# Block-sparse attention into an FFT-gated layer on one Trainium2 core: earlier masks, smaller transform steps, rationed loads, outputs turned by TensorE

## Chip, core and metric

The kernel runs on one core of one Trainium2 chip, in one launch. The metric is the device time of the whole program in microseconds (us), as a median over runs. The profile is of one execution on that core.

## What is computed

Two layers follow each other. The first is causal attention on 4 batches, 8 heads, 768 positions and head width 64, in which every query sees its own block of 64 keys and the best three blocks by a gate score (query times mean key of the block). The second takes the joined heads (768 x 512 per batch), projects them three ways, convolves the second projection with a filter over the sequence by an FFT, multiplies the three, and projects again:

```
gate_scores = einsum('bhsd,bhnd->bhsn', q, k_mean_of_block)      # causal blocks only
mask        = own block | top 3 blocks, and pos_q >= pos_k
attn        = softmax(where(mask, q @ k.T / sqrt(64), -1e9)) @ v
x           = attn, heads joined                                  # (4, 768, 512)
x1, x2, x3  = split(x @ w_proj, 3)
conv        = irfft(rfft(x2) * rfft(filter))                      # over the 768 positions
out         = (x1 * conv * x3) @ w_out
```

## The kernel before

**The unit of work.** Heads are taken in pairs: 16 pairs, numbered p, four to a batch. Each head's 768 x 768 causal scores are computed in three groups of 896 columns, so a pair has six groups and the program has 96 slots (`slots`), six to a pair and 24 to a batch. Slot n of the main loop (L642) issues, in this order: the score matmuls of slot n+1 (`scores`, L371), the exponential of slot n on ScalarE (L387, written `ex`) and its triangular cut on GpSimd (L390), the transfers that were put off (`flush`), the list `early[n]`, one step of the second layer, the product matmuls of slot n-1 with V (`products`, L396), further steps, and the list `bank[n]`. All engines run their instructions in the order in which the program issues them. Below, n0 = 6p is the first slot of pair p.

**Preparing a pair.** K and Q arrive as rows (`load`, L75) and are turned by TensorE (L269, tiles `kt`, `qt`). ScalarE casts them (L282 to `KH`, L316 to `TQ`); VectorE takes block sums of the keys (L285, `krs`), makes the gate's right side from them (`prep_kr`, L301 to L305, `bd` and `kr`) and keeps the rounding rest of the queries (L318, `ql`). `prep_gate` (L324) multiplies them into the gate scores `g`; `prep_mask` (L337) finds the third best per query on VectorE (L342, `m`) and writes 0/1 masks (`MN`). `prep_turn` (L350) turns the masks on TensorE (L354, `mt`) and ScalarE writes them as 44 extra rows beside the queries (L355, into `TQ`). The score matmuls then have 76 rows to sum over, 64 of the head and 12 of the mask (L378). The first head of a pair reads `TQ` and `KA`, the second `QB` and `KB`; SyncE's transfers copy `KH` into `KA` and `KB` (L291, L292) and the second head's rows from `TQ` into `QB` (L322 for the queries, L357 for the masks). L355 overwrites rows that L322 reads.

**Where these steps stand.** A table by slot sets it (L611 to L630): for p > 1 loads of k, q, v at n0-15, n0-13, n0-11, `prep_k` at n0-9 and n0-7, `prep_q` at n0-6 and n0-5, `prep_kr` at n0-5, `prep_gate` at n0-4, `prep_mask` at n0-3, `prep_turn` in `bank` of slot n0-2. The scores of slot n0 are issued at the start of slot n0-1, so on TensorE they come straight behind the turned masks.

**Out of the attention.** After a head's third group, VectorE divides by the sums (L416, L417, `xnat`). After a pair, a transposing transfer on SyncE's queue (L431) turns it to `xT`, and `fold` (L435, two VectorE operations, L438 and L439, at slot 6p+9) adds and subtracts the mirrored halves (`xf`). Only the last pair is turned by TensorE (L428, copied by ScalarE, L429).

**The second layer** (`hyena`, L442) of batch b runs as a list of steps in the slots of batch b+1, from the fifth on, each step with a cost in a credit scheme: six projections `x2` (L459), eight `gates` (x1 and x3, L518 and L521), three transforms `fft` (cosine and sine half, six matmuls into two PSUM tiles, then four VectorE products L477 to L481), four inverses and six outputs (L533). The last batch's list runs at the end, with nothing beside it, on the score tiles of PSUM (`sc_tile`, two buffers).

**The first batch** has no second layer beside it. Its slots from 2 on hold a list (`filler`, L559): cosines from sines, the filter folded (L227, fp32 matmuls, tile `rev`, into `fil`), its spectrum (`spectrum`, L245: six matmuls into two PSUM tiles, ScalarE scaling one and VectorE combining, L240 and L241, into `Asb`, `Bsb`, `A2`), and the turned transform matrices (L231). The six filter transfers (L210, L211) are issued before slot 0, the weights `wp` in four pieces in slots 2 to 8. The sine table itself is made before slot 0 (L114 to L136: products on TensorE, rounding on VectorE and GpSimd, a sum on VectorE, L131, sine on ScalarE, L132).

Of the kernel before, what the change touches and what calls it, by code (L numbers as in the profile page):

```python
# [18 lines left out]
def kernel(  # L19
# [43 lines left out]
    staging = ctx.enter_context(tc.tile_pool(name="staging", bufs=1))  # L63
# [60 lines left out]
    def sine_whole(i):  # L124
        pr, ka = sine[i]
        nc.gpsimd.tensor_scalar(ka, in0=ka, scalar1=-MAGIC, scalar2=-float(S2),
                                op0=ALU.add, op1=ALU.mult)

    def sine_rest(i):
        pr, ka = sine.pop(i)  # L130
        nc.vector.tensor_add(ka, pr, ka)  # L131
        nc.scalar.activation(FS[:, i, :], ka, AF.Sin, bias=0.0, scale=TWO_PI / S2)  # L132

    nc.scalar.activation(tw, twf, AF.Sin, bias=0.0, scale=math.pi / S)
    for i in range(HC):
        sine_products(i)  # L136
    sel = const.tile([P, 2], FP32, name="sel")
# [3 lines left out]
    for i in range(HC):  # L141
        sine_whole(i)
# [51 lines left out]

    sgn = const.tile([P, 1], FP32, name="sgn")
# [17 lines left out]
    def load_wp(dc):  # L213
        nc.gpsimd.dma_start(wp[:, dc, :], moe_w_proj[dc * P:(dc + 1) * P, :])
# [16 lines left out]
    def turn_matrix(dst, src, j):  # L231
        pt = one("pt", (P, HC, P), fp)
        for i in range(HC):
            nc.tensor.transpose(pt[:, i, :], src[:, i, P * j:P * (j + 1)], id16)
        (nc.scalar.copy if dst is IC else nc.vector.tensor_copy)(
            dst[:, j, :], pt.rearrange("p i t -> p (i t)"))

    def turned(dst, first, s0, second, s1, op):
# [6 lines left out]
    def spectrum(j, part):  # L245
        sl = slice(P * j, P * (j + 1))
        if part == 0:
            spec[j] = hcp, hsp = one("hcps"), one("hsps")
            for i in range(HC):
                nc.tensor.matmul(hcp, lhsT=FC[:, i, sl], rhs=fil[:, 0, i, :],  # L250
                                 start=(i == 0), stop=(i == HC - 1))
            for i in range(HC):
                nc.tensor.matmul(hsp, lhsT=FS[:, i, sl], rhs=fil[:, 1, i, :],
                                 start=(i == 0), stop=(i == HC - 1))
            turned(Asb[:, j, :], hcp, tw[:, 0, j:j + 1], hsp, tw[:, 1, j:j + 1], ALU.add)
            cosB = tw0[:, 0:1] if j == 0 else tw[:, 0, j:j + 1]
            turned(Bsb[:, j, :], hsp, cosB, hcp, tw[:, 1, j:j + 1], ALU.subtract)
            if j == 0:
                turned(A2, hcp, tw0[:, 0:1], hsp, tw0[:, 1:2], ALU.add)
# [13 lines left out]
    def prep_k(p, t):  # L273
# [14 lines left out]
        for f in ((cast, sums) if t == 0 else (sums, cast)):  # L288
            f()
# [8 lines left out]
    def prep_kr(p):  # L298
        krs = state.pop(("krs", p))
        bd = small.tile([P, 2, NB], FP32, name="bd", tag="bd")  # L300
        nc.vector.tensor_tensor(bd, krs.unsqueeze(1).to_broadcast([P, 2, NB]),  # L301
                                sel.unsqueeze(2).to_broadcast([P, 2, NB]), op=ALU.mult)
        kr = small.tile([P, 2, 2, NB], fp, name="kr", tag="kr")
        nc.vector.tensor_copy(kr[:, 0], bd)
        nc.vector.tensor_sub(kr[:, 1], bd, kr[:, 0])  # L305
# [90 lines left out]
    def products(n):  # L396
# [14 lines left out]
        if g == NS - 1:  # L411
# [8 lines left out]
            if h == 1:  # L420
# [4 lines left out]
                if p == NP - 1:  # L425
                    xt = one("xt", (P, S), fp)
                    for c in range(SC):
                        nc.tensor.transpose(xt[:, P * c:P * (c + 1)], xn[:, c, :], id16)  # L428
                    nc.scalar.copy(xT[:, dc, :], xt)  # L429
                else:  # L430
# [11 lines left out]
    def hyena(b, spread):  # L442
# [20 lines left out]
        def fft(j):  # L463
            x2eo, PQ = st["x2"], st["PQ"]
            sl = slice(P * j, P * (j + 1))
            xc, xs = two("xc", "xs")
# [3 lines left out]
            for i in range(HC):  # L470
                nc.tensor.matmul(xs, lhsT=FS[:, i, sl], rhs=x2eo[:, 1, i, :],
                                 start=(i == 0), stop=(i == HC - 1))
            t1 = hy2.tile([P, Dm], FP32, name="t1", tag="t1")
            t2 = hy2.tile([P, Dm], FP32, name="t2", tag="t2")
            t3 = hy2.tile([P, Dm], FP32, name="t3", tag="t3")
            t4 = hy2.tile([P, Dm], FP32, name="t4", tag="t4")
            nc.vector.tensor_mul(t1, xc, Asb[:, j, :])  # L477
            nc.vector.tensor_mul(t4, xc, Bsb[:, j, :])  # L478
# [237 lines left out]
```

## Time and profile before

| | us |
|---|---|
| median of 3 runs | 327.16 |
| lowest, highest | 324.58, 331.69 |
| the profiled execution, device time | 325.43 |
| the profiled execution, span from first to last instruction | 323.7 |
| busy in the span: TensorE / VectorE / ScalarE / GpSimd | 250.3 / 183.9 / 174.7 / 131.1 |

In the profile PE is TensorE's matmuls, PEld its weight loads, DVE VectorE, ACT ScalarE, POOL GpSimd, SP SyncE, and SPq or POOLq the transfers that SyncE's or GpSimd's queue issues. A wait is written as engine, tile and line, then what ended the wait. The busy share is an average over stages: the start, the 24 slots of the first batch, 72 slots with the second layer beside them, and the last batch's second layer by itself.

### The profile page before, as it was taken

The numbers are of one execution on the slowest core, as the hardware profiler recorded it, in microseconds if no ns is written. First come the engines' busy times: TensorE is split into PE (matmuls) and PEld (weight loads), VectorE is DVE, ScalarE is ACT, GpSimd is POOL, SyncE is SP. The second block draws the span as 40 slices with busy tenths as digits, with TensorE's granted clock in tenths as the row PEclk, the third lists the DMA queues.
The fourth block names the chain that finished last, engine by engine and source line by source line (L and its number), as shares of the span: only waits on it lengthen the run. The fifth ranks groups of instructions, "written<-read, shape, count | busy, mean of one in ns | idle before, by whom it ended". The sixth has DMA issues, their size and how long they took to land.

```text
span 323.7 us, 6068 instructions
## 1 busy us (share of the span) xinstructions
PE 250.3 (77%) x2171; PEld 154.0 (48%) x2171; DVE 183.9 (57%) x561; ACT 174.7 (54%) x277; POOL 131.1 (40%) x227
## 2 busy tenths in 40 slices
PE   5378657728698978897979778979897789888675
PEld 3254334516464545654545445546454455444332
DVE  3566256433463858585438676765386758136650
ACT  3551356727477445666965365759753566431224
POOL 6753012221331365464312555552226557203680
PEclk9996598966769999999999999999999999999999
DMA  9699648494584927262968262649640201310005
GB/s 172 108 261 225 143 90 167 94 181 101 121 187 85 140 53 156 55 138 54 258 168 160 53 130 56 138 81 258 175 100 4 61 4 25 132 67 0 2 0 194
DMA packets 96943, 37.20 MB, mean 115 GB/s; under 512 B 88785, under 2 KB 92561, under 8 KB 96913
## 3 DMA queue, kind: packets, MB, share of 16 engines
q1 hardware_dynamic: 95808, 34.72, 48.5%
q0 software_dynamic: 1104, 2.10, 3.9%
q8 instruction: 17, 0.28, 0.4%
q14 instruction: 14, 0.11, 0.1%
HBM read 24.64 MB, written 6.29 MB: 96 GB/s over the span
## 4 chain that ended last, share of the span: by engine, by line
PE 33%; DVE 25%; ACT 13%; issue 10%; DMA 6%; POOL 4%; DVEq 0%; POOLq 0%; ACTq 0%
PE sps L378 5%; PE op L533 5%; ACT ex L387 3%; ACT TQ L355 3%; DMA xT<-xnat 3%; PE x1p L518 3%; PE x3p L521 3%; PE o L408 3%; DVE gg L526 3%; PE x2p L459 3%; DVE t L477 2%; DVE t L478 2%; ACT KH L282 2%; DVE m L342 2%; DVE krs L285 2%
## 5 line engine op out<-in xcount | busy, mean ns | idle before, releaser
L390 POOL TENSOR_SCALAR_AFFINE_SELECT ex<-ex 128x256 f16<-128x256 f16 x96 | 40.8, 427 | 122.8 <-ACT ex L387 103.4
L387 ACT ACTIVATE ex<-sps 128x896 f16<-128x896 f32 x96 | 88.3, 925 | 1.4 <-PE sps L378 1.0
L408 PEld LDWEIGHTS <-ex 128*128 128x128 f16 x672 | 34.5, 102 | 32.3 <-DVE xnat L417 17.6
L408 PE MATMUL o<-V,ex 128*128 128x65 f16 x672 | 39.2, 200 | 11.0 <-DVE xnat L417 10.7
L378 PE MATMUL sps<-TQ,KA 76*128 76x512 f16 (+1 forms) x144 | 29.7, 322 | 21.9 <-ACT TQ L355 18.8
L282 ACT CAST KH<-kt 128x384 f16<-128x384 f32 x32 | 15.3, 478 | 46.0 <-DVE krs L285 25.0
L285 DVE TENSOR_REDUCE krs<-kt 128x6 f32<-128x384 f32 x32 | 17.5, 552 | 33.2 <-PE kt L269 27.3
L480 POOL TENSOR_TENSOR PQ<-t,t 128x512 f16<-128x512 f32 x12 | 15.2, 1265 | 41.1 <-DVE t L479 41.1
L378 PEld LDWEIGHTS <-KA 76*128 76x128 f16 x144 | 15.1, 106 | 33.1 <-issue 28.9
L378 PE MATMUL sps<-QB,KB 76*128 76x512 f16 (+1 forms) x144 | 28.1, 306 | 0.5 <-ACT ex L387 0.3
L355 ACT ACTIVATE TQ<-mt 44x768 f16<-44x768 f16 x16 | 12.9, 805 | 24.7 <-PE mt L354 18.5
L533 PE MATMUL op<-wo,yT 128*128 128x512 f16 x96 | 23.7, 379 | 2.0 <-POOL yT L489 2.0
L459 PE MATMUL x2p<-wp,xf 128*128 128x512 f16 x96 | 24.0, 379 | 1.1 <-DVE xf L438 0.8
L521 PE MATMUL x3p<-xT,wp 128*128 128x384 f16 x96 | 19.5, 325 | 4.8 <-ACT x1sb L524 3.4
L526 DVE TENSOR_TENSOR gg<-x1sb,x3p 128x384 f32<-128x384 f16 x24 | 13.2, 552 | 17.1 <-PE x3p L521 9.6
L518 PE MATMUL x1p<-xT,wp 128*128 128x384 f16 x96 | 19.5, 325 | 3.9 <-DVE t L478 3.9
L316 ACT ACTIVATE TQ<-qt 128x384 f16<-128x384 f32 x32 | 15.7, 497 | 11.2 <-PE qt L269 11.1
L489 POOL TENSOR_TENSOR yT<-gg,yy 128x384 f16<-128x384 f32 x16 | 15.9, 995 | 13.7 <-DVE yy L506 13.7
L269 PE MATMUL kt<-id,k_nat 128*128 128x128 f32 x96 | 19.3, 323 | 1.0 <-DMA k_nat<-in_k_dram 1.0
L318 DVE SCALAR_TENSOR_TENSOR ql<-qt,TQ 128x256 f16<-128x256 f32 (+1 forms) x32 | 15.4, 486 | 7.6 <-ACT TQ L316 7.6
L536 ACT COPY osb<-op 128x512 f32<-128x512 f32 x24 | 14.2, 590 | 10.1 <-PE op L533 10.1
L521 PEld LDWEIGHTS <-wp 128*128 128x128 f16 x128 | 12.4, 97 | 15.0 <-issue 7.3
(145 smaller groups left out, 487.9 us busy)
## 6 DMA issues: line engine op xcount, KB each, us to landing
k_nat<-in_k_dram SPq DMA_DIRECT2D x32, 192.0 KB
q_nat<-in_q_dram SPq DMA_DIRECT2D x32, 192.0 KB
v_nat<-in_v_dram SPq DMA_DIRECT2D x32, 192.0 KB
out_dram<-osb SPq DMA_DIRECT2D x24, 256.0 KB
KA<-KH SPq DMA_DIRECT2D x16, 96.0 KB
KB<-KH SPq DMA_DIRECT2D x16, 96.0 KB
QB<-TQ SPq DMA_DIRECT2D x16, 96.0 KB
wp<-in_moe_w_proj_dram POOLq DMA_DIRECT2D x4, 384.0 KB, 5.6
```

Of the source, the lines that this page charges most:

```text
L282: nc.scalar.copy(kh[:, F * t:F * (t + 1)], kt)
L285: nc.vector.tensor_reduce(out=krs[:, 6 * t:6 * t + 6], in_=kt.rearrange("p (n j) -> p n j", j=64), axis=AX.X, op=ALU.add)
L355: nc.scalar.activation(tq[64:108, :], mt[64:108].rearrange("p c s -> p (c s)"), AF.Copy, bias=0.0, scale=MQ)
L378: nc.tensor.matmul(t[:, col:col + q1 - q0], lhsT=kk[0:64 + NB, P * kc:P * (kc + 1)], rhs=qq[0:64 + NB, q0:q1], start=True, stop=True, skip ...
L387: nc.scalar.activation(ex, t[:, 0:W], AF.Exp, bias=0.0, scale=EXPS)
L390: nc.gpsimd.affine_select(out=tri, in_=tri, compare_op=ALU.is_ge, fill=0.0, base=0, pattern=[[0, 2], [1, P]], channel_multiplier=-1)
L408: nc.tensor.matmul(o[:, qc, :], lhsT=ex[:, c0:c0 + P], rhs=V16[p % 3][:, kc, h, 0:65], start=first, stop=False, skip_group_check=True)
L459: nc.tensor.matmul(pa, lhsT=xf[:, eo, dc, P * i:P * (i + 1)], rhs=wp[:, dc, Dm:2 * Dm], start=(dc == 0), stop=(dc == DC - 1))
L518: nc.tensor.matmul(x1p, lhsT=wp[:, d2, dsl], rhs=xT[:, d2, hs], start=(d2 == 0), stop=(d2 == DC - 1))
L521: nc.tensor.matmul(x3p, lhsT=wp[:, d2, 2 * Dm + P * dc:2 * Dm + P * (dc + 1)], rhs=xT[:, d2, hs], start=(d2 == 0), stop=(d2 == DC - 1))
L526: nc.vector.tensor_mul(g, x1sb, x3p)
L533: nc.tensor.matmul(op, lhsT=st["yT"][:, cc, P * i:P * (i + 1)], rhs=wo[:, cc, :], start=(cc == 0), stop=(cc == DC - 1))
```

## The change

It has six parts.

1. **Pair schedule.** `prep_k` at n0-10 and n0-8, `prep_q` at n0-7 and n0-6, `prep_kr` at n0-7 and (for p > 0) on GpSimd, gate and mask together at n0-5, `prep_turn` at n0-3; loads at n0-17, n0-13, n0-9; `fold` at 6p+10. Where VectorE and ScalarE both read a turned key tile, ScalarE's cast comes first (for p > 0).
2. **Transform in halves.** `fft(j)` becomes `fft(j, 0)` and `fft(j, 1)`, each with one PSUM tile and two VectorE products. In the last batch each half has a whole score tile.
3. **First batch's transfers.** Before slot 0 stand only k, v, q of the next pairs; the three pairs of filter transfers go to slots 2, 4, 6; `wp` goes in 12 pieces of one third, from slot 9 on; `wo` at slot 30.
4. **Filter spectrum in steps.** One half per slot is multiplied and copied out of PSUM (`hsb`), GpSimd scales and VectorE combines from these copies some slots later; the filler list becomes a table by slot. The staging tiles share memory with tiles of the second layer.
5. **First outputs turned by TensorE.** Pairs 0 to 3 take no transposing transfer; `turn_x` (slot 6p+8) turns them on TensorE and VectorE copies them out.
6. **Start.** The rounded part of the sine is added in PSUM by a matmul with a scaled identity (`idn`) and all three sines come before the first keys; `prep_kr(0)` stands before `prep_q(0)`.

```diff
@@ sine
-        nc.vector.tensor_add(ka, pr, ka)
-        nc.scalar.activation(FS[:, i, :], ka, AF.Sin, bias=0.0, scale=TWO_PI / S2)
+        kw = hy2.tile([P, F], fp, name="dft_kw", tag="x1sb")
+        nc.gpsimd.tensor_scalar(kw, in0=ka, scalar1=-MAGIC, scalar2=1.0, op0=ALU.add, op1=ALU.mult)
+        nc.tensor.matmul(pr, lhsT=idn, rhs=kw, start=False, stop=True, skip_group_check=True)
+        nc.scalar.activation(FS[:, i, :], pr, AF.Sin, bias=0.0, scale=TWO_PI / S2)
@@ spectrum
+    def spectrum(j, which):
+        sl = slice(P * j, P * (j + 1))
+        hps = one("hps")
+        for i in range(HC):
+            nc.tensor.matmul(hps, lhsT=(FC, FS)[which][:, i, sl], rhs=fil[:, which, i, :],
+                             start=(i == 0), stop=(i == HC - 1))
+        spec[j, which] = hsb = hy2.tile([P, Dm], FP32, name="hsb", tag=f"h{which}")
+        (nc.scalar.copy if which else nc.vector.tensor_copy)(hsb, hps)
...
+        nc.gpsimd.tensor_scalar(t, in0=second, scalar1=s1, scalar2=0.0, op0=ALU.mult, op1=ALU.add)
         nc.vector.scalar_tensor_tensor(out=dst, in0=first, scalar=s0, in1=t, op0=ALU.mult, op1=op)
@@ prep_kr
+        e = nc.gpsimd if p else nc.vector
...
@@ turn_x
+    def turn_x(p):
+        b, dc = divmod(p, DC)
+        xn, xT = xns[p], xTs[b]
+        xt = one("xt", (P, S), fp)
+        for c in range(SC):
+            nc.tensor.transpose(xt[:, P * c:P * (c + 1)], xn[:, c, :], id16)
+        (nc.scalar.copy if p == NP - 1 else nc.vector.tensor_copy)(xT[:, dc, :], xt)
@@ fft
+            xx = single("xx")
             for i in range(HC):
-                nc.tensor.matmul(xc, lhsT=FC[:, i, sl], rhs=x2eo[:, 0, i, :],
+                nc.tensor.matmul(xx, lhsT=(FC, FS)[which][:, i, sl], rhs=x2eo[:, which, i, :],
...
@@ table by slot
-            at(early, n0 - 15, lambda p=p: load(p, "k"))
-            at(early, n0 - 11, lambda p=p: load(p, "v"))
-            at(bank, n0 - 9, lambda p=p: prep_k(p, 0))
...
-        at(early, n0 - 5, lambda p=p: prep_kr(p))
-        at(bank, n0 - 4, lambda p=p: prep_gate(p))
-        at(early, n0 - 3, lambda p=p: prep_mask(p))
-        at(bank, n0 - 2, lambda p=p: prep_turn(p))
-        at(early, n0 + 3, lambda p=p: fold(p - 1))
+            at(early, n0 - 17, lambda p=p: load(p, "k"))
+            at(early, n0 - 9, lambda p=p: load(p, "v"))
+            at(bank, n0 - 10, lambda p=p: prep_k(p, 0))
...
+            at(early, n0 - 7, lambda p=p: prep_kr(p))
+            at(bank, n0 - 5, lambda p=p: gate_mask(p))
+            at(bank, n0 - 3, lambda p=p: prep_turn(p))
+        if p < DC:
+            at(bank, n0 + 8, lambda p=p: turn_x(p))
+        at(early, n0 + 10, lambda p=p: fold(p))
+        fills[10 + 2 * j].append(lambda j=j: filter_fold(j))
+        fills[16 + 4 * j].append(lambda j=j: spectrum(j, 0))
+        fills[17 + 4 * j].append(lambda j=j: spectrum(j, 1))
```

**TensorE at the end of the mask turn of a pair in the second batch, before.** `MN` are the masks, `KA` and `TQ` the first head's keys and queries, and the three score matmuls are those of the pair whose masks were just turned.

```order
L354 LDWEIGHTS MN_159
L354 MATMUL mt<-id_171,MN_159 128x128
L378 LDWEIGHTS KA_164
L378 MATMUL sps<-TQ_168,KA_164 128x512
L378 LDWEIGHTS KA_164
L378 MATMUL sps<-TQ_168,KA_164 128x128
L378 LDWEIGHTS KA_164
L378 MATMUL sps<-TQ_168,KA_164 128x256
```

The same place now; `KB` and `QB` belong to the second head of the pair before:

```order
L361 LDWEIGHTS MN_167
L361 MATMUL mt<-id_179,MN_167 128x128
L385 LDWEIGHTS KB_173
L385 MATMUL sps<-QB_177,KB_173 128x384
L385 LDWEIGHTS KB_173
L385 MATMUL sps<-QB_177,KB_173 128x128
L385 LDWEIGHTS KB_173
L385 MATMUL sps<-QB_177,KB_173 128x384
```

A whole slot of other work (another pair's scores, a step of the second layer, products) now stands between the turned masks and the scores that read them.

**SyncE's queue behind the first pair's query copy, before.** `fa` and `fb` are the filter's halves, `KA_164` to `QB_170` the second pair's operands.

```order
L357 DMA QB_169<-TQ_167 12x768
L80 DMA v_nat<-in_v_dram 128x6x64 x2
L210 DMA fa<-in_moe_filter_fft_dram 128x512
L211 DMA fb<-in_moe_filter_fft_dram 128x512
L210 DMA fa<-in_moe_filter_fft_dram 128x512
L211 DMA fb<-in_moe_filter_fft_dram 128x512
L210 DMA fa<-in_moe_filter_fft_dram 128x512
L211 DMA fb<-in_moe_filter_fft_dram 128x512
L80 DMA k_nat<-in_k_dram 128x6x64 x2
L80 DMA q_nat<-in_q_dram 128x6x64 x2
L291 DMA KA_164<-KH_200 64x768
L292 DMA KB_166<-KH_200 64x768
```

The same place now, as far as the second pair's query copy (`QB_178`, L329):

```order
L79 DMA k_nat<-in_k_dram 128x6x64 x2
L79 DMA v_nat<-in_v_dram 128x6x64 x2
L79 DMA q_nat<-in_q_dram 128x6x64 x2
L364 DMA QB_177<-TQ_175 12x768
L297 DMA KA_172<-KH_209 64x768
L298 DMA KB_174<-KH_209 64x768
L79 DMA k_nat<-in_k_dram 128x6x64 x2
L329 DMA QB_178<-TQ_176 64x768
L211 DMA fa<-in_moe_filter_fft_dram 128x512
L212 DMA fb<-in_moe_filter_fft_dram 128x512
```

The six filter transfers and one load moved from ahead of the second pair's operands to behind its query copy.

## Rows read from the trace of the kernel before

**Rows 1.** The page, 40 equal slices: granted clock, share of the DMA engines.
```profile
PEclk9996598966769999999999999999999999999999
DMA  9699648494584927262968262649640201310005
```

**Rows 2.** Timeline of ACT (start, us, engine, line; in brackets the wait before).
```profile
15.83 0.92 ACT L387 ACTIVATE ex<-sps 128x896 f16<-128x896 f32 x1 [0.99 <-PE sps L378]
...
34.35 0.81 ACT L355 ACTIVATE TQ<-mt 44x768 f16<-44x768 f16 x1 [5.21 <-DMA QB<-TQ]
...
73.47 0.81 ACT L355 ACTIVATE TQ<-mt 44x768 f16<-44x768 f16 x1 [6.37 <-PE mt L354]
...
89.61 0.92 ACT L387 ACTIVATE ex<-sps 128x896 f16<-128x896 f32 x1
...
273.70 0.92 ACT L387 ACTIVATE ex<-sps 128x896 f16<-128x896 f32 x1
```

**Rows 3.** Windows: stretch, length, busy PE, PEld, DVE, ACT, POOL, granted clock, DMA.
```profile
15.83:89.61 73.78, 48.31 (x428) 32.79 (x427) 35.78 (x126) 37.13 (x56) 19.84 (x40) 0.78 0.75 154
89.61:96.00 6.39, 6.24 (x63) 4.63 (x61) 4.21 (x21) 4.68 (x9) 2.55 (x5) 0.59 0.80 175
96.00:273.70 177.70, 151.82 (x1441) 94.29 (x1439) 115.40 (x348) 109.82 (x175) 79.44 (x117) 1.00 0.50 108
```

**Rows 4.** Waits of PE, 96 to 275 us (in total, times, longest).
```profile
PE sps L378 <- ACT TQ L355: 10.7, 11, 1.2
PE x1p L518 <- DVE t L478: 3.9, 6, 0.8
...
PE ye L498 <- DVE lt L345: 1.8, 2, 0.9
PE x3p L521 <- DVE t L481: 1.0, 3, 0.3
```

**Rows 5.** The chain that ended last, in order of time (start, us, what).
```profile
28.46 5.79 DMA QB<-TQ
...
62.53 6.93 DMA xT<-xnat
```

**Rows 6.** Transfers from 8 to 20 us, in 40 slices.
```profile
GB/s 217 219 218 218 219 215 220 216 242 226 257 143 164 108 67 21 0 0 0 0 0 0 0 0 0 0 0 31 31 22 141 207 281 261 257 221 186 219 266 410
```

**Rows 7.** Instructions by line and form, whole span (busy us, mean ns, idle before).
```profile
L461 DVE CAST x2eo<-x2p 128x512 f16<-128x512 f32 x12 | 8.3, 688 | 5.9 <-PE x2p L459 5.9
...
L304 DVE CAST kr<-bd 128x24 f16<-128x24 f32 x16 | 4.5, 279 | 0.5
...
L126 POOL TENSOR_SCALAR dft_ka<-dft_ka 128x384 f32<-128x384 f32 x3 | 1.5, 509 | 0.9 <-DVE dft_ka L120 0.8
...
L429 ACT COPY xT<-xt 128x768 f16<-128x768 f16 x1 | 0.8, 798 | 1.0 <-PE xt L428 1.0
...
L428 PE MATMUL xt<-id,xnat 128*128 128x128 f16 x6 | 0.5, 221 | 0.9 <-DVE xnat L417 0.9
```

**Rows 8.** Timeline: the fold's first operation early, and late with POOL beside it.
```profile
53.62 0.35 DVE L438 TENSOR_TENSOR xf<-xT 128x384 f16<-128x384 f16 x1
...
271.05 0.99 POOL L489 TENSOR_TENSOR yT<-gg,yy 128x384 f16<-128x384 f32 x1 [0.96 <-DVE yy L506]
...
271.35 0.92 DVE L438 TENSOR_TENSOR xf<-xT 128x384 f16<-128x384 f16 x1
```

**Rows 9.** Timeline of the start, PE and POOL.
```profile
10.47 0.40 PE L333 MATMUL g<-kr,TQ 128*128 128x24 f16 x2 [2.28 <-DVE kr L304]
...
11.39 0.82 POOL L173 TENSOR_SCALAR_AFFINE_SELECT KA<-KA 12x768 f16<-12x768 f16 x1
...
14.89 0.59 PE L378 MATMUL sps<-TQ,KA 76*128 76x512 f16 x1 [0.95 <-ACT TQ L355]
```

**Rows 10.** Timeline of DVE in the last batch's second layer.
```profile
302.19 0.69 DVE L477 TENSOR_TENSOR t<-sps,Asb 128x512 f32<-128x512 f32 x1 [1.15 <-PE sps L471]
```

**Rows 11.** Waits of DVE, 100 to 275 us.
```profile
DVE krs L285 <- PE kt L269: 19.7, 5, 4.8
```

More of the change, by code (lines that the diff above doesn't have):

```diff
@@ L136 @@
         sine_products(i)
+    idn = const.tile([P, P], fp, name="idn")
+    nc.gpsimd.tensor_scalar(idn, in0=id32, scalar1=-float(S2), scalar2=0.0, op0=ALU.mult, op1=ALU.add)
+    for i in range(HC):
+        sine_rest(i)
     sel = const.tile([P, 2], FP32, name="sel")
@@ L234, in turn_matrix @@
             nc.tensor.transpose(pt[:, i, :], src[:, i, P * j:P * (j + 1)], id16)
[L235 to L238 removed]
+        nc.vector.tensor_copy(dst[:, j, :], pt.rearrange("p i t -> p (i t)"))
+    spec = {}
+    def spectrum(j, which):
+        sl = slice(P * j, P * (j + 1))
+        hps = one("hps")
+        for i in range(HC):
+            nc.tensor.matmul(hps, lhsT=(FC, FS)[which][:, i, sl], rhs=fil[:, which, i, :],
+                             start=(i == 0), stop=(i == HC - 1))
+        spec[j, which] = hsb = hy2.tile([P, Dm], FP32, name="hsb", tag=f"h{which}")
+        (nc.scalar.copy if which else nc.vector.tensor_copy)(hsb, hps)
@@ L241, in turned @@
         nc.vector.scalar_tensor_tensor(out=dst, in0=first, scalar=s0, in1=t, op0=ALU.mult, op1=op)
-    spec = {}
[L245 to L259, printed above, removed]
@@ L287, in sums @@
                                     axis=AX.X, op=ALU.add)
-        for f in ((cast, sums) if t == 0 else (sums, cast)):
-            f()
+        if p == 0 and t == 0:
+            sums()
+            state["cast"] = cast
+        else:
+            cast()
+            sums()
+            if p == 0:
+                state.pop("cast")()
         if t == 1:
@@ L424, in products @@
                 xT, xf = xTs[b], xTs["f", b]
[L425 to L430, printed above, removed]
+                if p >= DC and p < NP - 1:
                     late.append(lambda: nc.sync.dma_start_transpose(
@@ L557, in make_flip @@
             fill=1.0, base=-(P - 1), pattern=[[1, P]], channel_multiplier=1)
-    def filler():
-        first = [lambda: cosines()]
-        first += [lambda i=i: filter_fold(i) for i in range(HC)]
-        first += [lambda j=j: spectrum(j, 0) for j in range(HC)]
-        first += [lambda j=j: (turn_matrix(IC, FC, j), turn_matrix(IS, FS, j)) for j in range(HC)]
-        return first
     def flush():
@@ L573 @@
     prep_k(0, 1)
-    flush()
-    sine_rest(0)
+    prep_kr(0)
     prep_q(0, 0)
     prep_q(0, 1)
+    nc.scalar.preload_act_table_set("natural_log_exp_and_others")
+    prep_gate(0)
+    prep_mask(0)
     flush()
-    sine_rest(1)
-    prep_kr(0)
-    prep_gate(0)
-    sine_rest(2)
-    nc.vector.memset(MN[0], 0.0)
-    prep_mask(0)
-    nc.scalar.preload_act_table_set("natural_log_exp_and_others")
+    load(2, "k")
+    load(1, "v")
+    load(2, "q")
     prep_turn(0)
-    flush()
     nc.gpsimd.tensor_copy(KB[0][64:64 + NB, :], erow)
@@ L590 @@
     prep_v(0)
-    load(1, "v")
-    for i in range(HC):
-        load_filter(i)
     scores(0)
@@ L651 @@
             queue += hyena(b - 1, True)
-        if b == 0:
-            if m >= 2 and spread_filler:
-                spread_filler.pop(0)()
-        else:
+        for f in fills[n]:
+            f()
+        if b:
             credit += 28.2 / per * 1.03
```

125 lines of the change are left out of this document (74 added, 51 removed).

## Prediction

> **What bounds the kernel now.** I read the page's slices first. In [rows 1] the granted TensorE clock is below full speed only in the first twelve slices, the start and the first batch; from then on it is full. So the time is not of one kind, and I cut it by the exponentials, of which there is one per slot: slot 0 begins at 15.83 us, slot 24 at 89.61, slot 95 at 273.70 [rows 2]. The first 24 slots take 73.8 us, 3.07 each, the other 72 take 184.1 us, 2.56 each, although only the latter have the second layer beside them. The rest is 15.8 us of start and 50.0 us of tail (323.7 - 273.70).
>
> The windows say what each stretch lacks [rows 3]. In the first batch no engine is full: TensorE is busy 48.3 of 73.8 us, and that at a mean clock of 0.78; ScalarE 37.1, VectorE 35.8. It is bound by waits. The two longest on ScalarE are of the masks' writing: 5.2 us until the second pair's query copy has landed, and 6.4 us until a mask turn is done [rows 2]. The chain says what lies behind them [rows 5]: that copy took 5.8 us on its way, behind the filter in SyncE's queue, and a transposing transfer took 6.9 us; `fold` waits for such a transfer in VectorE's queue, and `prep_mask` stands behind `fold`. From 96 us on TensorE is busy 151.8 of 177.7 us, 85%: it is the bound, and what can go is its waits. The largest is the one for the masks, 10.7 us in 11 waits of about 1 us [rows 4].
>
> **The change part by part.** The sum is made against the profiled execution: 325.43 us, of which 323.7 are span and 1.7 lie around it. It is 1.7 us below the median of the runs, 327.16, and I add that at the end.
>
> *Start.* The gate waits 2.3 us for the first pair's `kr`, which VectorE makes after two sine operations and the query rests [rows 9]. Now it comes before these. Three small matmuls and two sines on ScalarE come ahead of the first keys instead. The scores of slot 0, at 14.89 us, also need the key rows that GpSimd finishes at 12.2 (11.39 + 0.82), so no more than 2.3 us can go, and a loss of 1 us is possible if the sines hold up the key cast. I take -1.0.
>
> *First batch.* What it would take if no wait stood out is bounded by work. TensorE's 48.3 us at a clock of 0.78 are 37.7 at full clock (an estimate: not all of a matmul's time goes with the clock); three outputs turned by six transposes, 0.5 us each time [rows 7], make it 39.2. VectorE: 35.8, less four times three small `kr` operations (0.28 the longest kind), 3.3, plus three copies of a turned output, 0.8 each by ScalarE's row, plus three copies of half a spectrum, 0.69 each by that of `x2eo` [rows 7]: 37.0. ScalarE loses seven scalings and gains three copies, and stays below. At the 85% that TensorE reaches later the batch would take 39.2 / 0.854 = 45.9 us. The other floor is the transfers. The window moved 154 GB/s for 73.8 us [rows 3], 11.4 MB; saturated by the same kind of loads the queue moved 215 to 220 GB/s [rows 6], so these bytes need 52 us. Three transposing transfers leave and one load goes ahead of slot 0, but the loads of the next pairs stay. The ends are thus 45.9 and, if nothing comes of it, 73.8; I take 53, next to the floor of the transfers: -20.8. The named waits fit this. The second pair's query copy is now behind one load instead of three filter pairs and two loads, so the 5.2 us go; the transposing transfer, and with it the 6.4 us, is gone; mask, fold and turn stand in different slots. Late next is the wait for the transfers themselves.
>
> *Slots 24 to 95.* Between the mask turn and the scores that read it TensorE now has a slot of other work, some 2.5 us against a wait of 1; ScalarE's 0.8 us for L355 falls in it. All 10.7 us of [rows 4] are open; some will come back as waits for ScalarE and VectorE, which are reached later than TensorE in each slot, and I keep 8. The waits for the transform's products (3.9 and 1.0) shrink because each half gives its one PSUM tile back after two products instead of four: I keep 2.5. Of the 1.8 us behind the mask's `lt` I keep 1. In the 6.4 us from 89.61 the clock was 0.59 [rows 3]; 6.24 busy us there are 3.7 at full clock, 4.3 at 85%: -2. Against this, the fold of a batch's last pair now stands in the slot of the first `x2` step, which TensorE reaches before VectorE is done: three times one or two operations, 0.35 us each alone and 0.92 beside GpSimd [rows 8], so 0.4 to 1.8 us; I take 1.2, +3.6. `prep_kr` on GpSimd is not in the trace: three operations of 0.28 us on VectorE, at most 0.5 (the larger tile of L126) on GpSimd, twelve pairs; GpSimd is busy 45% of the stretch, and the gate comes two slots later, so nothing. If that cover failed it would be up to 1.5 us a pair, 18 us. Sum -9.9, say -10, with ends of 0 and -16.
>
> The Trainium skill speaks against two of these moves (page "SBUF — State Buffer", section "SBUF: two separate sides"): VectorE and GpSimd share one port pair, a VectorE operation with two SBUF inputs and a GpSimd operation lock each other out for a whole instruction. Seven spectrum operations now read both inputs from SBUF, and their partner moved to GpSimd. The trace agrees with the rule, the 0.35 us against 0.92 of [rows 8]. By it each of the seven could wait for one GpSimd scaling, an estimate of 0.7 us, and the sum would be 4.8 us longer; without it, nothing. TensorE and the transfers are the floor there, so my sum has nothing for it.
>
> *Tail.* VectorE is the bound in the three transforms at the end, and waits before the second and third: 1.15 us in [rows 10], 1.1 in the other like it, because a transform's first product waits for both halves. With halves it can begin after three matmuls of six. Half a score tile is given away by each, so the ring turns faster: 0 to -2.3, I take -1.5.
>
> Sum: 325.4 - 1.0 - 20.8 - 10 - 1.5 = 292.1, and with 1.7 for the median 293.8: **294 us**.
>
> **The rivals.** *The clock stays low in the first batch.* The clock fell after stretches in which TensorE stood idle [rows 1, 3]. If the first batch keeps such gaps, its 39.2 us of work at full clock become up to 78 at half, and the batch takes its 73.8 us as before: 294 + 20.8 = 315. For it: without the second layer TensorE has 39 us of work in 53, less than later. Against it: the gaps of several microseconds are those that have names above, and the change removes what they wait for.
>
> *The waits only change their names.* The mask's place behind other work is of use only if no other wait is nearly as late. ScalarE casts, scales and exponentiates in order, VectorE drains in order, and in each slot both come after TensorE. If the slot is paced by these, the first batch's 20.8 and the 8 of the masks come back: 294 + 28.8 = 323, no change. For it: in the first batch three engines are within a few per cent of each other in work. Against it: all three are half idle there.
>
> *Slower: VectorE stands before the gate.* `prep_mask` now follows `prep_gate` in the same slot, so VectorE's next instruction waits until TensorE has come through a step, the products and the gate. Behind it in VectorE's queue stand the drains of the next slot, which give TensorE its PSUM tiles back. The price is a wait like that for turned keys, 19.7 us in 5, 3.9 each [rows 11], put on TensorE twelve times: 47 us, against 33 gained, which gives 294 + 47 = 341. It decides from 2.8 us a pair on (33 / 12). Against it: those 19.7 us stood in the trace while TensorE was 85% busy, so VectorE waits ahead of TensorE, not behind it.
>
> **How the numbers follow.** The forecast with its own range, 280 to 307, has 0.68; the low clock, 315, has 0.14; changed names, 323, 0.06; VectorE before the gate, 0.06; better than 280 (the first batch at 46 and all later waits gone: 325.4 - 2.3 - 27.9 - 16 - 2.3 + 1.7 = 279), 0.06. The range from 280 to 315 leaves out 0.18. A measurement of this kernel can tell about 2% from no change, so "faster" begins below 320.6: 0.68 + 0.14 + 0.06 = 0.88; same 0.06; slower 0.06.
>
> **What would show it.** In the profile after: slot 24's exponential at about 68 us; no wait of 5 us before L355's successor in the first batch; a granted clock of 0.9 or more there; the wait of the score matmuls for the masks' writing under 3 us in all; about 2.4 us a slot from slot 24 on; a new wait of `x2p` for `xf` three times. I am wrong if the first batch still takes over 65 us, if the later slots keep 2.56 us, or if the mask search waits for the gate by more than a microsecond a pair.

## Result, and the profile after

The changed kernel took 289.38 us, the median of four runs (287.29 to 290.83), against 328.75 for the kernel before in the same comparison: a ratio of 0.8875, with its 95% interval [0.8764, 0.8986]. The same file run again in a later comparison took 285.17 (284.17 to 291.76), ratio 0.8722 [0.8674, 0.8769]. Forecast were 294 us and a range of 280 to 315. The profiled execution took 290.83 us, of which 289.1 are span.

The stretches are cut as before, by the exponentials of slots 0, 24, 48 and 95. This table carries the rest of the text (us; "again" is the same kernel's second profile):

| | before | forecast of the change | after | change | again |
|---|---|---|---|---|---|
| start, to slot 0 | 15.83 | -1.0 | 15.71 | -0.1 | 15.45 |
| first batch, slots 0 to 23 | 73.8 | -20.8 | 53.5 | -20.3 | 51.5 |
| slots 24 to 95 | 184.1 | -10 | 166.7 | -17.4 | 166.6 |
| of these, slots 48 to 95 | 120.2 | | 105.6 | -14.6 | 105.6 |
| tail, from slot 95 | 50.0 | -1.5 | 53.2 | +3.2 | 50.2 |
| span | 323.7 | | 289.1 | -34.6 | 283.7 |

The page's slices of after, which answer to [rows 1]:

```profile
PEclk9997988977779999999999999999999995999998
DMA  9997898997907965568774735796512011300005
```

The granted clock still dips in the first twelve slices, and there is a new dip in slice 34, at the start of the tail, where before had none. The timeline of ScalarE answers to [rows 2]:

```profile
13.91 0.81 ACT L362 ACTIVATE TQ<-mt 44x768 f16<-44x768 f16 x1 [2.88 <-DMA QB<-TQ]
...
15.71 0.92 ACT L394 ACTIVATE ex<-sps 128x896 f16<-128x896 f32 x1 [0.99 <-PE sps L385]
...
38.93 0.81 ACT L362 ACTIVATE TQ<-mt 44x768 f16<-44x768 f16 x1 [2.33 <-DMA QB<-TQ]
...
69.19 0.91 ACT L394 ACTIVATE ex<-sps 128x896 f16<-128x896 f32 x1
...
235.91 0.92 ACT L394 ACTIVATE ex<-sps 128x896 f16<-128x896 f32 x1
```

The masks' writing (L355 before, L362 now) waited 5.21 and 6.37 us in the first batch; the longest left are 2.88, in the start, and 2.33. The windows answer to [rows 3] (columns: length, busy PE, PEld, DVE, ACT, POOL, granted clock, DMA share, GB/s):

```profile
15.71:69.19 53.48, 43.09 (x436) 30.85 (x435) 33.48 (x118) 33.01 (x50) 26.72 (x61) 0.87 0.85 168
69.19:130.33 61.14, 53.95 (x524) 35.16 (x522) 42.77 (x125) 38.53 (x63) 35.75 (x62) 0.94 0.65 126
75.54:235.91 160.37, 150.43 (x1472) 96.99 (x1468) 111.49 (x331) 110.79 (x177) 87.86 (x152) 0.98 0.57 126
130.33:235.91 105.58, 100.20 (x996) 64.16 (x995) 72.91 (x217) 75.87 (x122) 56.91 (x101) 1.00 0.54 128
235.91:246.00 10.09, 7.43 (x44) 3.41 (x44) 2.19 (x6) 3.47 (x6) 2.33 (x4) 0.68 0.13 52
```

For slots 48 to 95 the row of before is

```profile
153.54:273.70 120.16, 103.30 (x990) 64.23 (x987) 77.43 (x237) 75.92 (x121) 53.46 (x80) 1.00 0.49 113
```

There TensorE's idle time fell from 16.9 us (120.16 - 103.30) to 5.4 (105.58 - 100.20): it is 95% busy now, at the upper level of its clock (2.4 GHz) in both. Its waits from 75.54 us on, which answer to [rows 4]:

```profile
PE x2p L469 <- DVE xf L448: 2.7, 3, 2.2
PE x3p L533 <- ACT x1sb L536: 1.7, 3, 0.6
PE op L545 <- POOL yT L501: 1.7, 2, 0.9
PE sps L385 <- ACT ex L394: 1.6, 3, 0.7
PE o L415 <- DVE xnat L424: 1.5, 3, 0.5
```

The wait for the masks, 10.7 us in 11 before, is not in the list any more, nor are those for the transform's products. The wait of `x2p` for the fold (`xf`) is there three times, as forecast.

### The profile page after: what moved, and what is told of

The parts are those of the page before. It is cut to its first block, busy times and chain, and to the rows that moved or that the text cites. A ratio compares the mean times of both kernels' runs of the same rounds, so it can differ in the third digit from the quotient of the medians.

```text
span 289.1 us, 6157 instructions
## 1 busy us (share of the span) xinstructions
PE 245.6 (85%) x2198; PEld 153.9 (53%) x2198; DVE 176.3 (61%) x523; ACT 170.4 (59%) x270; POOL 148.7 (51%) x288
## 4 chain that ended last, share of the span: by engine, by line
PE 56%; DVE 12%; ACT 11%; POOL 9%; issue 5%; DMA 5%; SPq 1%; ACTq 0%; DVEq 0%; POOLq 0%
PE sps L385 8%; PE op L545 7%; PE x2p L469 6%; PE x3p L533 5%; PE o L415 5%; PE x1p L530 5%; ACT ex L394 4%; DMA QB<-TQ 3%; PE kt L269 3%; PE qt L269 3%; PE xx L481 3%; ACT TQ L362 2%; POOL yT L501 2%; DVE xnat L424 2%; DMA k_nat<-in_k_dram 2%
## 5 line engine op out<-in xcount | busy, mean ns | idle before, releaser
L397 POOL TENSOR_SCALAR_AFFINE_SELECT ex<-ex 128x256 f16<-128x256 f16 x96 | 39.9, 418 | 84.5 <-ACT ex L394 78.4
L415 PEld LDWEIGHTS <-ex 128*128 128x128 f16 x672 | 33.8, 100 | 25.0 <-DVE xnat L424 9.4
L415 PE MATMUL o<-V,ex 128*128 128x65 f16 x672 | 37.9, 198 | 5.7 <-DVE xnat L424 5.1
L385 PE MATMUL sps<-TQ,KA 76*128 76x512 f16 (+1 forms) x144 | 28.4, 310 | 4.9 <-DMA k_nat<-in_k_dram 2.1
L492 POOL TENSOR_TENSOR PQ<-ta 128x512 f16<-128x512 f32 x12 | 15.2, 1269 | 31.3 <-DVE ta L491 31.2
L545 PE MATMUL op<-wo,yT 128*128 128x512 f16 x96 | 26.4, 411 | 4.3 <-POOL yT L501 4.3
L469 PE MATMUL x2p<-wp,xf 128*128 128x512 f16 x96 | 25.5, 390 | 3.6 <-DVE xf L448 3.6
L536 ACT CAST x1sb<-x1p 128x384 f16<-128x384 f32 x24 | 11.6, 483 | 15.0 <-PE x1p L530 14.9
L362 ACT ACTIVATE TQ<-mt 44x768 f16<-44x768 f16 x16 | 12.9, 806 | 12.0 <-DMA QB<-TQ 6.7
L269 PE MATMUL qt<-id,q_nat 128*128 128x128 f32 x96 | 18.5, 309 | 0.3 <-ACT KH L282 0.3
```

What stands on the lines that cost most here:

```text
L269: nc.tensor.transpose(y[:, P * c:P * (c + 1)], x[:, HC * t + c].rearrange("p h d -> p (h d)"), id32)
L362: nc.scalar.activation(tq[64:108, :], mt[64:108].rearrange("p c s -> p (c s)"), AF.Copy, bias=0.0, scale=MQ)
L385: nc.tensor.matmul(t[:, col:col + q1 - q0], lhsT=kk[0:64 + NB, P * kc:P * (kc + 1)], rhs=qq[0:64 + NB, q0:q1], start=True, stop=True, skip ...
L397: nc.gpsimd.affine_select(out=tri, in_=tri, compare_op=ALU.is_ge, fill=0.0, base=0, pattern=[[0, 2], [1, P]], channel_multiplier=-1)
L415: nc.tensor.matmul(o[:, qc, :], lhsT=ex[:, c0:c0 + P], rhs=V16[p % 3][:, kc, h, 0:65], start=first, stop=False, skip_group_check=True)
L469: nc.tensor.matmul(pa, lhsT=xf[:, eo, dc, P * i:P * (i + 1)], rhs=wp[:, dc, Dm:2 * Dm], start=(dc == 0), stop=(dc == DC - 1))
```

## Experiments

No kernel leaves out work. "First two" are slots 0 to 47; the slots 48 to 95 are the quiet stretch, where the first batch's transfers and fillers are over.

| run | what differs | median | ratio [95%] | first two | 48 to 95 |
|---|---|---|---|---|---|
| before | | | | 137.7 | 120.2 |
| after / again | | 289.38 / 285.17 | 0.8875 [0.8764, 0.8986] / 0.8722 [0.8674, 0.8769] | 114.6 / 112.5 | 105.6 / 105.6 |
| e1 | turn a slot later | 295.00 | 0.8978 [0.8922, 0.9035] | 117.3 | 110.8 |
| e2 | transposing transfers back | 291.83 | 0.8896 [0.8845, 0.8947] | 118.6 | 105.6 |
| e3 | filter loads first | 286.56 | 0.8745 [0.8685, 0.8804] | 112.2 | 105.6 |
| e4 | transform whole | 287.74 | 0.8761 [0.8715, 0.8808] | 113.1 | 106.1 |
| e6 | schedule alone, on before | 303.69 | 0.9267 [0.9198, 0.9335] | 128.9 | 107.8 |
| e7 | old order of casts | 292.91 | 0.8987 [0.8930, 0.9044] | 114.9 | 108.3 |
| e8 | old spectrum | 286.92 | 0.8779 [0.8729, 0.8828] | 111.2 | 105.6 |
| e9 | old transfers | 288.91 | 0.8864 [0.8806, 0.8922] | 115.1 | 105.6 |
| e10 | filler slots early again | 289.97 | 0.8903 [0.8849, 0.8958] | 117.0 | 105.6 |
| e11 | e9 and e10 together | 286.91 | 0.8807 [0.8765, 0.8850] | 110.9 | 105.6 |
| e12 | last fold sooner, one load later | 285.89 | 0.8785 [0.8737, 0.8834] | 114.2 | 104.7 |

In the seven kernels that change nothing of the quiet stretch (after, twice, e2, e3, e8 to e11) it took 105.56 to 105.60 us. So half a microsecond there is an effect. In the first two batches the two profiles of one kernel differ by 2.1 us, and in the tail by 3.0; less than that says nothing.

**e1, the mask turn a slot later.** On after:

```diff
-            at(bank, n0 - 3, lambda p=p: prep_turn(p))
+            at(bank, n0 - 2, lambda p=p: prep_turn(p))
```

> The changed kernel with one edit: the mask turn goes back from slot n0-3 to slot n0-2, straight before the scores that read it; everything else stays. If the place of the turn is what the later slots gained (their wait for the masks' writing went from 10.7 us to nothing), the wait comes back with about 1 us for each of the 12 pairs after the first batch: 8 to 12 us more than the changed kernel, some 299 us, nearly all of it in slots 24 to 95. If the gain came from other parts (halved transforms, the order of casts, the fold's new place) and the wait for the masks only hides another as late, it costs 3 us or less.

The quiet stretch became 5.2 us longer (110.78 - 105.58), and this wait of TensorE came back in it:

```profile
PE sps L385 <- ACT TQ L362: 4.2, 6, 0.9
```

So the place of the turn is worth 5.2 us in 47 slots, by the mechanism named; over slots 24 to 95 it is 7.0 (173.7 against 166.7), less than the 8 to 12 expected.

**e2, the transposing transfers of pairs 0 to 3 put back.**

```diff
-                if p >= DC and p < NP - 1:
+                if p < NP - 1:
...
-        if p < DC:
-            at(bank, n0 + 8, lambda p=p: turn_x(p))
```

> The changed kernel with the outputs of the first four pairs turned by SyncE's transposing transfers again, as in the kernel before; mask, fold and turn keep their new slots. If the 6.9 us of a transposing transfer counted only because fold waited for it and the mask search stood behind fold, the new slots already cure that: 0 to 3 us more than the changed kernel. If the transposing transfers themselves held up the first batch (time on the transfer engines, or the copies of keys and queries behind them in the queue), it costs 5 us or more, in the first 24 slots, and waits for landings of KA, KB or QB grow there.

The first two batches took 118.6 us, 4 to 6 more than with the outputs turned by TensorE. In the first batch alone it was 55.1 us, 1.6 to 3.7 more, so neither expectation came as it stands. The longest wait of the masks' writing there was 3.70 us.

**e3, the six filter loads before slot 0.**

```diff
+    for i in range(HC):
+        load_filter(i)
...
-    for i in range(HC):
-        early[2 + 2 * i].append(lambda i=i: load_filter(i))
```

> The changed kernel with the six filter transfers issued before slot 0 again, behind the next loads and ahead of the second pair's copies. If the order in SyncE's queue is what made slot 5 late before, the second pair's query copy lands some 5 us later, the exponential of slot 4 comes 4 to 7 us later, and 3 to 6 us of this are left at slot 24, since the slots behind it have fewer bytes to wait for. If the transfers are a floor by their sum alone, the order does not matter: at slot 24 there is 1 us or less of difference.

No loss: 50.4 us for the first batch, in which the masks' writing waited 0.8 us at most. That the filter stood ahead of the second pair's copies is not what the change gains from.

**e4, the transform whole again.**

```diff
-        def fft(j, which):
+        def fft(j):
...
-            xx = single("xx")
+            xc, xs = two("xc", "xs")
...
```

> The changed kernel with the transforms of the second layer whole again (six matmuls into two PSUM tiles, four VectorE products), in the batches' slots and in the tail. If the halves removed the waits of x1 and x3 for the transform's products (4.9 us in the kernel before), slots 24 to 95 become 3 to 5 us longer, and the tail 0 to 2 us longer, because there a first product waits for both halves: 3 to 7 us in all. If the freed PSUM tiles only move the wait to another step, under 1.5 us in all.

The quiet stretch took 106.09, 0.5 more; the tail 50.0, against 50.2 for after run again. The halves are worth almost nothing. In the tail they traded one wait for another. VectorE before its product in e4 (the 1.15 us of [rows 10]), and then in after before the gate's product that now comes ahead of it:

```profile
258.71 0.69 DVE L490 TENSOR_TENSOR t<-sps,Asb 128x512 f32<-128x512 f32 x1 [1.08 <-PE sps L484]
...
262.82 0.69 DVE L490 TENSOR_TENSOR t<-sps,Asb 128x512 f32<-128x512 f32 x1 [1.16 <-PE sps L484]
```

```profile
262.79 0.55 DVE L538 TENSOR_TENSOR gg<-x1sb,sps 128x384 f32<-128x384 f16 x1 [0.94 <-ACT x1sb L536]
263.26 0.68 DVE L486 TENSOR_TENSOR ta<-sps,Asb 128x512 f32<-128x512 f32 x1
...
267.14 0.68 DVE L486 TENSOR_TENSOR ta<-sps,Asb 128x512 f32<-128x512 f32 x1
```

One transform follows the other after 3.9 us (267.14 - 263.26), in e4 after 4.1 (262.82 - 258.71).

**e5, the changed kernel once more**, without an edit, to see how far one profile can be trusted.

> The changed kernel itself once more, nothing changed but an empty line, as the measure beside the other three of this set and for how much its stretches vary from one execution to the next. Two kernels whose first 24 slots were the same but for small things took 49.9 and 53.5 us there, so I expect 50 to 54 us in the first batch, 166 to 169 in slots 24 to 95, 50 to 53 in the tail, and 286 to 291 us in all. If the first batch comes out near 53.5 again, the earlier filter transfers (50.4) were a real gain; if it comes out near 50, they were not.

Its tail settles the +3.2. Here are the window of the tail's first 10 us and, from the timeline of TensorE, the last 20 of the third batch's 24 output matmuls, first in again, then in after (whose window stands above, 235.91:246.00):

```profile
233.47:244.00 10.53, 7.87 (x60) 4.07 (x60) 2.19 (x6) 5.24 (x9) 2.34 (x4) 1.00 0.30 115
...
238.42 4.48 PE L546 MATMUL op<-wo,yT 128*128 128x512 f16 x20
```

```profile
241.12 7.05 PE L545 MATMUL op<-wo,yT 128*128 128x512 f16 x20
```

The same twenty matmuls took 4.48 us at a granted clock of 1.00, and 7.05 where the window shows 0.68. That is 2.6 of the 3.0 us between the two tails. The other profiles agree: the tail took 50.0 to 50.3 us where the clock in its first 10 us was 1.00, 51.5 to 52.0 at 0.83 and 53.1 at 0.68. So the longer tail is the clock, not the program. TensorE's wait just before the outputs is 0.88 us in both, so why it comes in one execution and not in the other stays open.

**e6, the pair schedule alone, on the kernel before** (the loads of k, preparation, gate, mask, turn and fold at the new places; the old order of casts, and all else as before):

```diff
-            at(bank, n0 - 9, lambda p=p: prep_k(p, 0))
+            at(bank, n0 - 10, lambda p=p: prep_k(p, 0))
...
+        at(bank, (n0 - 5) if p > 1 else 2, lambda p=p: (prep_gate(p), prep_mask(p)))
...
+        at(bank, n0 - 3, lambda p=p: prep_turn(p))
```

> The kernel before with the pair schedule alone: keys, queries, gate, mask and turn one or two slots sooner, k loads two slots sooner, fold one slot later; its transposing transfers, early filter transfers, whole transforms, old spectrum, order of casts and kr on VectorE stay. If the schedule is the heart of the change in both stretches, the first batch loses 10 us or more of its 73.8 (mask no longer behind fold, turn no longer behind the mask) and the later slots 10 us or more of 184: 300 to 307 us. If the schedule gives only what its undoing cost (5.6 us), the time is near 321 us and the rest belongs to the other parts.

```profile
15.83:87.82 71.99, 49.12 (x421) 32.21 (x420) 37.23 (x129) 37.24 (x57) 19.35 (x40) 0.74 0.82 155
87.82:144.76 56.94, 52.16 (x519) 33.53 (x518) 43.48 (x131) 37.73 (x62) 28.36 (x43) 1.00 0.64 123
144.76:252.51 107.75, 100.95 (x991) 64.39 (x989) 79.96 (x235) 74.51 (x120) 53.22 (x80) 1.00 0.54 126
```

It gives 12.4 us of the quiet stretch's 14.6 and 7.0 of the second batch (63.9 - 56.9), but in the first batch only 1.8 (73.8 - 72.0). The masks' writing still waited there, longer than the 5.21 of [rows 2]. ScalarE's row, and two of SyncE's queue:

```profile
35.95 0.81 ACT L355 ACTIVATE TQ<-mt 44x768 f16<-44x768 f16 x1 [6.71 <-DVE kr L304]
```

```profile
28.08 3.75 SPq L80 DMA_DIRECT2D k_nat<-in_k_dram  x2
31.92 0.64 SPq L322 DMA_DIRECT2D QB<-TQ  x1
```

The profile names `kr` on VectorE, which ended last; the query copy, issued at 31.92 behind a key load that took 3.75 us to issue, may have been as late. In either case the schedule alone leaves the first batch its long waits.

**e7, VectorE's block sums ahead of ScalarE's cast again, for the second half of a pair's keys.**

```diff
-            cast()
-            sums()
+            for f in ((cast, sums) if t == 0 and p else (sums, cast) if p else (cast, sums)):
+                f()
```

> The changed kernel with the old order on the second half of a pair's keys: VectorE's block sums before ScalarE's cast, for every pair but the first. In the kernel before, ScalarE stood 25 us waiting for these sums. If that standing held up exponentials and through them TensorE, the later slots get 3 to 6 us longer and the wait of KH for krs comes back with 10 us or more. If ScalarE had the time to stand (it is busy 69% of the stretch), under 1.5 us in all.

The quiet stretch took 108.34, 2.8 us more, and ScalarE has a wait again that after lacks. In that stretch of before, then of e7:

```profile
ACT KH L282 <- DVE krs L285: 9.8, 7, 3.3
...
ACT KH L282 <- DVE krs L285: 6.4, 6, 1.6
```

The prediction had no price for this edit.

**e8, the old spectrum**: two PSUM tiles at once, ScalarE scaling, VectorE combining from PSUM.

```diff
-        nc.gpsimd.tensor_scalar(t, in0=second, scalar1=s1, scalar2=0.0, op0=ALU.mult, op1=ALU.add)
+        nc.scalar.activation(t, second, AF.Copy, bias=0.0, scale=s1)
```

> The changed kernel with the old spectrum: for each of the three parts both halves in one slot (slots 16, 20, 24), ScalarE scaling from PSUM and VectorE combining straight behind it. In the kernel before, TensorE waited 5.3 us for these scalings and VectorE 6.8. If they were part of what bound the first batch, it gets 3 to 6 us longer than in the run of the changed kernel beside it. If the transfers or other waits are the floor there, the difference is under 1.5 us.

The first two batches took 111.2 us, no more than the 112.5 to 114.6 of after. The small steps buy nothing. The combining operations of after, and GpSimd's scaling (columns: busy us, mean ns, idle before):

```profile
L259 DVE SCALAR_TENSOR_TENSOR Asb<-hsb,tw,turn 128x512 f16<-128x512 f32 x3 | 2.7, 888 | 5.8 <-POOL turn L258 5.8
...
L259 DVE SCALAR_TENSOR_TENSOR Bsb<-hsb,tw,turn 128x512 f16<-128x512 f32 x3 | 2.2, 745 | 0.6 <-POOL turn L258 0.6
...
L258 POOL TENSOR_SCALAR turn<-hsb,tw 128x512 f32<-128x512 f32 x7 | 4.8, 688 | 0.0
```

```profile
L244 DVE SCALAR_TENSOR_TENSOR Asb<-hcps,tw,turn 128x512 f16<-128x512 f32 x3 | 2.2, 750 | 5.2 <-ACT turn L243 5.2
L244 DVE SCALAR_TENSOR_TENSOR Bsb<-hsps,tw,turn 128x512 f16<-128x512 f32 x3 | 2.2, 750 | 2.3 <-ACT turn L243 2.3
```

From SBUF, with GpSimd as partner, three operations took 888 ns in place of 750 and three 745: 0.4 us in all, and VectorE's idle time before them is no longer (6.4 against 7.5 us). The mean of 888 is made of two operations of 0.95 to 0.96 us and one of 0.75.

**e9, the old order of loads; e10, the fillers in the early slots again; e11, both.** e9 puts `wp` in four pieces into slots 2 to 8, the filter loads before slot 0, and the pairs' loads at n0-15, n0-13 and n0-11; e10 changes the fillers' slots, with the filter loads before slot 0:

```diff
-        fills[10 + 2 * j].append(lambda j=j: filter_fold(j))
-        fills[16 + 4 * j].append(lambda j=j: spectrum(j, 0))
+        fills[3 + j].append(lambda j=j: filter_fold(j))
+        fills[6 + j].append(lambda j=j: spectrum(j, 0))
...
```

> The changed kernel with the old order of all loads: before slot 0 only the next values and the six filter transfers, keys and queries of the third pair from slot 0 on, keys at n0-15 and values at n0-11, the weights in four whole pieces in slots 2 to 8, the output weights in slot 12. The filter work stays spread as in the change. If the first batch's gain is the rationing of transfers (filter and weights together; the filter alone did nothing), slot 12 comes 8 us or more later than at 42 us and the first batch is 60 us or more. If the gain is the spreading of the filter work, the first batch stays under 56 us.

> The changed kernel with the filter work in the old slots: folds in slots 3 to 5, both halves of a spectrum in each of slots 6 to 8, combined two slots later, the turned matrices in 9 to 11; the filter transfers stand before slot 0, as they must then. Weights and other loads stay rationed. If it is the crowding of filter work into slots 2 to 11 that cost the first batch, slot 12 comes 8 us or more later than at 42 us and little of that is won back: 60 us or more in the first batch. If it is the transfers, slot 12 comes 3 us or less later and the first batch stays under 56 us.

> Both edits together: old order of loads and old slots of the filter work. With the pair schedule alone the first batch took 72.0 us, with the whole change 51 to 54, and no part undone by itself cost more than 3 us there. If one of the two carries the gain, this run's first batch is that run's, within 2 us. If each covers for the other (work that waits for a late transfer only where both are early), it is 8 us or more above the larger of the two.

Windows of the first and second batch in e10, then in e11:

```profile
15.52:74.93 59.41, 44.75 (x441) 31.91 (x440) 38.80 (x123) 33.81 (x50) 30.47 (x67) 0.76 0.74 148
74.93:132.56 57.63, 51.83 (x520) 34.08 (x518) 39.95 (x120) 37.55 (x62) 32.18 (x56) 0.96 0.77 137
```

```profile
15.99:74.21 58.22, 45.68 (x441) 31.93 (x440) 38.56 (x123) 33.92 (x50) 28.34 (x59) 0.85 0.85 163
74.21:126.89 52.68, 49.60 (x520) 32.88 (x518) 39.61 (x120) 37.68 (x62) 30.62 (x56) 1.00 0.63 131
```

Early fillers lengthened the first batch to 59.4 us and shortened the second to 57.6; beside the old loads they took the first from 55.2 (e9) to 58.2 and the second from 60.0 to 52.7. Early fillers beside the new loads cost 2.4 to 4.5 us over the two batches (117.0); with both undone they take 110.9 us together, no more than after's 112.5 to 114.6. So rationing the loads and spreading the fillers move time over the border between the batches and gain nothing in sum.

**e12, the fold of a batch's last pair a slot sooner, and one query load behind the first pair's copies.**

```diff
-    load(1, "q")
...
+    load(1, "q")
     load(2, "k")
...
-        at(early, n0 + 10, lambda p=p: fold(p))
+        at(early, n0 + (9 if p % DC == DC - 1 else 10), lambda p=p: fold(p))
```

> The changed kernel with two edits in different stretches. The second pair's queries are loaded behind the first pair's copies of keys and queries instead of ahead of them: the mask's writing before slot 0 waited 2.9 us for the query copy to land, so slot 0 begins 1 to 2 us sooner, at 13.5 to 14.5 us, if that is what holds the start; if the key rows from GpSimd hold it, under 0.5 us. And the last pair of each batch is folded one slot sooner: the first projection's wait for the fold, 2.7 us in 3 in slots 24 to 95, goes, which takes 1.5 to 3 us off those slots, or nothing if the next wait is as late. In all 2 to 4 us under the changed kernel, 282 to 286 us.

The quiet stretch took 104.68, 0.9 less, but slots 24 to 95 together 167.7, no less than the 166.6 to 166.7 of after. Slot 0 came at 14.54 us, 0.9 to 1.2 sooner, and the masks' writing no longer waited for a transfer:

```profile
12.74 0.81 ACT L361 ACTIVATE TQ<-mt 44x768 f16<-44x768 f16 x1 [2.06 <-PE mt L360]
14.54 0.92 ACT L393 ACTIVATE ex<-sps 128x896 f16<-128x896 f32 x1 [0.99 <-PE sps L384]
```

In all, 285.89 us is not to be told from 285.17, so no version is shown to beat the changed kernel.

## Why the prediction was right, and where not

**The whole.** Faster, 294 forecast, 285 to 289 measured. The mechanism held: waits went, TensorE is the bound, and no rival came. That the total came so near is in part luck: slots 24 to 95 gave 7.4 us more than forecast, start and tail 5.6 less. Against "the waits only change their names" stand TensorE's 95% in slots 48 to 95 and e1. The clock in the first batch is 0.87, not a half. The signs named in advance came too (slot 24 at 69.19 and 66.90, 166.7 us for 71 slots, 2.35 each; the 2.56 of before is 184.1 divided by 72, by 71 it is 2.59), but for the first batch's clock, a little under the 0.9 asked for. VectorE does not stand before the gate: from 100 to 236 us its wait of the mask search is 1.3 us in 2, and the largest are for ScalarE:

```profile
DVE krs L285 <- ACT KH L282: 11.3, 11, 2.3
...
DVE m L349 <- PE g L340: 1.3, 2, 0.6
```

**Slots 24 to 95: -17.4 where -10 was forecast; this is the sum that failed.** Its largest term was right: of the masks' 10.7 us, 8 were kept, and e1 gives 7.0. Three others were not. The halves were to bring 2.5 us; e4 shows 0.5 in slots 48 to 95. The fold in the slot of `x2` was to cost 3.6; its wait is 2.7 in three, 2.2 of it at the first, and e12 gives 0.9 back for the two later folds. The clock was to bring 2 us behind slot 24. It did rise there (1.00 in the first 6 us of after and 0.78 of again, against 0.59), yet slots 24 to 28 took 16.4 us in place of 10.4. With the old loads (e9) they took 16.0, with the old slots of the fillers (e10) 9.3: the fillers' new slots, which reach to slot 28, cost some 6 us there, and the other slots, 29 to 95, gained 23.4 (173.7 to 150.3). The step left out was the order of casts: 2.8 us in slots 48 to 95 by e7. The rest is in the schedule: alone it gives 12.4 there, of which e1 explains 5.2, and 19.4 in slots 24 to 95 (184.1 - 164.7), more than the whole change, since e6 leaves the fillers in their early slots. The forecast let the separation of mask, fold and gate count in the first batch only. That it is this which brings the other 7 is argued; no run moved it by itself.

**First batch: the size right (-20.3, or -22.3 by the second profile's 51.5), the reasons half wrong.** The floor of 52 us for transfers fell: the window moved 168 GB/s for 53.48 us, 9.0 MB and not 11.4, 41 us at the 218 GB/s of [rows 6]. So that 20.8 came out is in part luck. The reason "the filter stands ahead of the copy" fell with e3. Nor was the second pair's query copy left with one load ahead of it: k, v and q of the next pairs only went from behind the first pair's mask copy to ahead of it, and still stand ahead of the second pair's copies. (That mask copy, of 12 rows, L357 and L364, is what the text over the queue's listings calls the first pair's query copy.) The 6.4 us were put down to the transposing transfer; with it back in e2 no wait of the masks' writing is over 3.7, so they were not its alone. Some of the first batch's gain is work moved into the second, as e11's 58.2 and 52.7 against 53.5 and 61.1 show, so the sum over both is what counts: 137.7 before, 128.9 with the schedule alone, 110.9 with everything but the loads' and fillers' new places. Those 18 us (128.9 - 110.9) come from what is left: outputs turned by TensorE (4 to 6 by e2), the order of casts (0 to 2 by e7), `kr` on GpSimd (no run moved it by itself), the spectrum, the halves, the start. Taken singly they give less than 18, and how it splits stays open.

**Start: -0.1 where -1.0 was forecast.** The gate's wait for `kr`, 2.28 us in [rows 9], did go. But the step named the key rows and the sines as what could hold slot 0, and not the first pair's query copy, which came last:

```profile
9.97 3.83 DMA QB<-TQ
```

It is issued when it was before (9.97 against 9.95 us) and behind the same loads, but lands at 13.80, while before all transfers had landed by 12.8 (the zeros in [rows 6]). New are three loads that are issued right behind it, from 10.57 us on; that they made it late is argued. e12, which takes a load away from ahead of the copy, brought slot 0 forward by 0.9 to 1.2 us, so the copy is what held it. One more sentence of that part was loose: "no more than 2.3 us can go"; the key rows at 12.2 would have allowed 2.7.

**Tail: +3.2 where -1.5 was forecast.** The clock made the 3 us (e5). At full clock the tail took 50.2 us, before 50.0, so the change brings nothing there: the halves gave 0.2 a transform, and e4 without them 50.0. The term had taken VectorE's wait for its product as free to go, where ScalarE's cast of the gate was nearly as late.

**What hides an edit.** No wait of TensorE for `kr` on GpSimd is among the largest of after, so its cover held, as forecast. The seven spectrum operations were the place where the Trainium skill (page "SBUF — State Buffer", section "SBUF: two separate sides") spoke for 4.8 us: VectorE and GpSimd lock each other out of a shared port pair. The trace of after agrees with the rule in kind: beside the three `Asb` operations GpSimd cut an exponential (`ex`) in 0.68 to 0.69 us, where all others took 0.40 to 0.49. One of the three:

```profile
58.20 0.95 DVE L259 SCALAR_TENSOR_TENSOR Asb<-hsb,tw,turn 128x512 f16<-128x512 f32 x1 [1.42 <-POOL turn L258]
...
58.73 0.69 POOL L397 TENSOR_SCALAR_AFFINE_SELECT ex<-ex 128x256 f16<-128x256 f16 x1
```

No scaling ran beside any of the seven. Two of the three took 0.2 us more than the 750 ns of e8, the third did not, and why stays open; at 0.4 us in all the measurement decides.

## What to carry to other kernels

Cut the time into stretches, and compare a change over a stretch long enough that work moved over its border is inside: here the first batch alone showed 5 us for a reordering that brought nothing over two. A consumer that follows its producer directly on the busiest engine is worth moving one step away, and so is the order in which two engines read one tile. When a wait is struck out, look for the second latest input of that instruction before counting the whole wait.

## What was not expected of the hardware

The quiet stretch repeats to 0.04 us in eight profiles (105.56 to 105.60), so there one profile resolves half a microsecond. The tail of one program does not: 50.2 or 53.2 us, by a granted clock of 1.00 or 0.68 in its first 10 us.
